# The first batch's q and k on one load queue, or on two

## The chip, the cores and the metric

The kernel runs on one core of one Trainium2 chip. A core has five engines that run side by side, each with its own instruction order: TensorE (PE, matmuls; its weight loads are listed as PEld), VectorE (DVE), ScalarE (ACT), GpSimd (POOL) and SyncE (SP), which here only issues transfers. Transfers between the main memory and the on-chip memory run on 16 DMA engines; SP and ScalarE each have a queue to them, called q1 and q10 in the profile. The metric is the device time of one execution in microseconds, the median of several.

## The reference

Linear attention with the map phi(x) = elu(x) + 1, and then a two-layer network with the tanh form of GELU:

```python
def phi(x):
    return np.where(x > 0, x, np.exp(x) - 1.0) + 1.0
q_p, k_p = (phi(q), phi(k))                       # q, k, v: 8 x 8 x 576 x 64, float32
kv = np.einsum('bhsd,bhse->bhde', k_p, v)
z = np.sum(k_p, axis=2)
num = np.einsum('bhsd,bhde->bhse', q_p, kv)
den = np.einsum('bhsd,bhd->bhs', q_p, z)[..., None] + 1e-06
x = num / den                                     # then heads side by side: 4608 x 512
h = x @ w_in                                      # w_in: 512 x 2048
g = 0.5 * h * (1.0 + np.tanh(c * (h + 0.044715 * h * h * h)))
return g @ w_out                                  # w_out: 2048 x 512
```

phi is computed as min(exp(x), max(x + 1, 1)): exp on ScalarE, the linear part and the minimum on VectorE.

## The kernel before

The order of instructions on each engine is the order in which the program names them; tiles come from pools, and an instruction waits for what it reads and for the tile it overwrites. Loads go through a pool of seven tiles (`pld`), so later loads wait until earlier tiles have been read.

The loads at the start, batch 0 first. Each of q and k comes in two halves:

```python
    def load_pairs(name, src, b, us=slice(0, NP), queue=nc.sync):
        s = src[b].rearrange("h s d -> (h s d)").rearrange("(u n f) -> n u f", n=P, f=J * D)
        queue.dma_start(out=ld[name, b][:, us, :], in_=s[:, us, :])

    def load_q_paired(b, parities=(0, 1)):
        src = q[b, :, 0:MAIN, :].rearrange("(u a) (p c) d -> p a u (c d)", a=2, c=C)
        for a in parities:
            nc.sync.dma_start(out=ld["q", b][:, NP * a : NP * (a + 1), :], in_=src[:, a])
    # ... cut ...
    halves = (slice(0, 2), slice(2, 4))
    for n in "qkv":
        ld_tile(n, 0)
    for s in range(2):
        load_q_paired(0, (s,))
        load_pairs("k", k, 0, halves[s], nc.scalar)
    nc.scalar.preload_act_table_set("exp_and_others")
    for s in range(2):
        load_pairs("v", v, 0, halves[s])
    for i in range(4):
        load_w(w_in_r, i)
    load_w(w_out_r, 0)
    # ... cut: batch 1's q, k and v, with w_out's other blocks between them, then batches 2 and 3 ...
```

A row of q's load is 256 floats (1 KB) long, a row of k's or v's 576 floats (2.3 KB).

The first batch, which fills the time until TensorE's main work can begin. `keep_warm` issues matmuls without use, to keep TensorE busy:

```python
    def first_batch():
        # ... cut ...
        keep_warm(18)
        for s in range(2):
            for n, hs in (("q", qs[s]), ("k", halves[s])):
                exp_of(n, 0, hs)       # ScalarE
                linear_of(n, 0, hs)    # VectorE, max(x + 1, 1)
                least_of(n, 0, hs)     # VectorE, the minimum
        transpose_q(0, nc.scalar.copy)
        keep_warm(10)
        transpose_q(1, nc.scalar.copy)
        keep_warm(2)
        for ii in range(2):
            cast_v_paired(0, halves[ii], nc.vector.tensor_copy)
        for ii in range(2):
            kv_ps = [bank("kv_ps", [P, E]) for _ in range(2)]
            kv_paired(0, ii, lambda a, ii: kv_ps[a])
            # ... cut: kv copied out of the accumulators by VectorE and ScalarE ...
        gelu_table()
        for s in range(2):
            cast_w_in(0, nc.gpsimd.tensor_copy, slice(256 * s, 256 * s + 256))
        for i in range(1, 4):
            cast_w_in(i, nc.gpsimd.tensor_copy)
        # ... cut: w_out's first blocks, then n, x, its transposes, and the first h quarters ...
```

Batch 1 is prepared while TensorE works on batch 0. In it stands the cast of the first part of w_out's last block, on VectorE, ahead of kv's copies:

```python
        def kv():
            kv_ps = [bank("kv_ps", [P, 2, E]) for _ in range(2)]
            for ii in range(2):
                kv_paired(b, ii, lambda a, ii: kv_ps[a][:, ii, :])
            cast_w_out(3, nc.vector.tensor_copy, slice(0, 1))
            for a, fn in enumerate((nc.vector.tensor_copy, nc.scalar.copy)):
                kv_evac(b, slice(2 * a, 2 * a + 2), kv_ps[a], fn)

        def last_w_out():
            cast_w_out(3, nc.scalar.copy, slice(1, 2))
            cast_w_out(3, nc.gpsimd.tensor_copy, slice(2, 4))
```

After that each batch is 16 blocks of h (`h_ps`, four matmuls each) with their GELU, and 16 groups of four matmuls into `o_ps`, with the next batch's attention between them.

Of the kernel before, what the change touches and what calls it, by code (L numbers as in the profile page):

```python
# [15 lines left out]
def kernel(  # L16
# [15 lines left out]
    nc = tc.nc  # L32
# [8 lines left out]
    NP = H // 2  # L41
# [40 lines left out]
    ld = {}  # L82
# [3 lines left out]
        shape = [P, NP, J * D] if b in PAIRED and name != "q" else [P, H, C * D]  # L86
        ld[name, b] = pld.tile(shape, FP32, name=name + "_x", tag="ld")

    def load_pairs(name, src, b, us=slice(0, NP), queue=nc.sync):
        s = src[b].rearrange("h s d -> (h s d)").rearrange("(u n f) -> n u f", n=P, f=J * D)  # L90
        queue.dma_start(out=ld[name, b][:, us, :], in_=s[:, us, :])

    def load_q_paired(b, parities=(0, 1)):
        src = q[b, :, 0:MAIN, :].rearrange("(u a) (p c) d -> p a u (c d)", a=2, c=C)
        for a in parities:
            nc.sync.dma_start(out=ld["q", b][:, NP * a : NP * (a + 1), :], in_=src[:, a])
# [45 lines left out]
    def cast_w_out(i, fn, ms=slice(0, 4)):  # L142
# [2 lines left out]
            in_=w_st[False, i][:, ms],  # L145
        )

    halves = (slice(0, 2), slice(2, 4))
    for n in "qkv":
        ld_tile(n, 0)  # L150
    for s in range(2):
        load_q_paired(0, (s,))
        load_pairs("k", k, 0, halves[s], nc.scalar)
    nc.scalar.preload_act_table_set("exp_and_others")
    for s in range(2):
        load_pairs("v", v, 0, halves[s])
    for i in range(4):
# [4 lines left out]
    load_w(w_out_r, 1)  # L162
    ld_tile("k", 1)
    load_pairs("k", k, 1)
    load_w(w_out_r, 2)
    ld_tile("v", 1)
# [581 lines left out]
```

## Time and profile before

| what | value |
|---|---|
| time, median of 3 | 289.38 us (289.31 to 289.49) |
| span of the profiled execution | 287.7 us, granted TensorE clock 1.000 |
| idle time of VectorE until the first q landed | 5.0 us |
| idle time of ScalarE for q's two landings | 3.8 us |
| transfers over the span | 53.76 MB, mean 187 GB/s |

The page's slices of 7.2 us each show how the time is divided. The digits are the busy share in tenths, the last line is the rate of transfers:

```profile
PE   8689999999999999999999999999999999999994
...
GB/s 241 407 407 396 410 400 263 348 219 153 184 231 279 228 174 167 380 148 139 204 296 202 79 257 349 106 78 169 34 49 30 88 66 0 50 92 6 0 73 73
```

TensorE is full from the fourth slice on. The transfers run at about 400 GB/s from the second slice to the sixth, that is to about 43 us: until then everything that is loaded lands one after the other at that rate, and later they are well below it.

### The profile page before, as it was taken

The numbers are of one execution on the slowest core, as the hardware profiler recorded it, in microseconds if no ns is written. First come the engines' busy times: TensorE is split into PE (matmuls) and PEld (weight loads), VectorE is DVE, ScalarE is ACT, GpSimd is POOL, SyncE is SP. The second block draws the span as 40 slices with busy tenths as digits, with TensorE's granted clock in tenths as the row PEclk, the third lists the DMA queues.
The fourth block names the chain that finished last, engine by engine and source line by source line (L and its number), as shares of the span: only waits on it lengthen the run. The fifth ranks groups of instructions, "written<-read, shape, count | busy, mean of one in ns | idle before, by whom it ended". The sixth has DMA issues, their size and how long they took to land.

```text
span 287.7 us, 4540 instructions
## 1 busy us (share of the span) xinstructions
PE 277.2 (96%) x1839; PEld 137.0 (48%) x1868; DVE 107.6 (37%) x180; ACT 164.5 (57%) x226; POOL 18.5 (6%) x25
## 2 busy tenths in 40 slices
PE   8689999999999999999999999999999999999994
PEld 3364455545445445544554455444544444444443
DVE  1950375733865283545146615540412010000001
ACT  3767896695975854585367735772562275027400
POOL 5067230000000000000000000000000000000000
PEclk9999999999999999999999999999999999999999
DMA  7999999965978888955799489825131220120022
GB/s 241 407 407 396 410 400 263 348 219 153 184 231 279 228 174 167 380 148 139 204 296 202 79 257 349 106 78 169 34 49 30 88 66 0 50 92 6 0 73 73
DMA packets 71379, 53.76 MB, mean 187 GB/s; under 512 B 42048, under 2 KB 62784, under 8 KB 71360
## 3 DMA queue, kind: packets, MB, share of 16 engines
q1 hardware_dynamic: 68112, 43.40, 54.1%
q10 hardware_dynamic: 3248, 10.09, 9.5%
q8 instruction: 14, 0.23, 0.3%
q14 instruction: 5, 0.04, 0.0%
HBM read 36.70 MB, written 9.44 MB: 160 GB/s over the span
## 4 chain that ended last, share of the span: by engine, by line
PE 92%; DVE 3%; DMA 2%; issue 1%; ACT 1%; DVEq 0%
PE o_ps L642 43%; PE h_ps L349 43%; PE n_ps L294 3%; DMA q_x<-in_q_dram 2%; PE kv_ps L278 1%; PE t_ps L341 1%; DVE k_p L236 1%; DVE q_p L236 0%; DVE k_p L223 0%; DVE vp L241 0%; PE kv_ps L263 0%; ACT q_e L212 0%; PE t_ps L469 0%; DVE x L330 0%; DVE x L309 0%
## 5 line engine op out<-in xcount | busy, mean ns | idle before, releaser
L642 PE MATMUL o_ps<-w_out_sb,g 128*128 128x512 bf16 (+1 forms) x581 | 126.3, 373 | 0.8 <-issue 0.2
L349 PE MATMUL h_ps<-xt,w_in_sb 128*128 128x512 bf16 (+1 forms) x556 | 116.7, 356 | 1.1 <-ACT xt L342 0.2
L359 ACT ACTIVATE g<-h_ps 128x512 bf16<-128x512 f32 x144 | 84.8, 597 | 46.8 <-PE h_ps L349 43.4
L642 PEld LDWEIGHTS <-g 128*128 128x128 bf16 x592 | 57.6, 98 | 65.2 <-issue 0.2
L349 PEld LDWEIGHTS <-w_in_sb 128*128 128x128 bf16 x636 | 57.4, 98 | 59.7 <-issue 0.9
L608 ACT COPY o_sb<-o_ps 128x512 f32<-128x512 f32 (+1 forms) x19 | 10.9, 575 | 61.3 <-PE o_ps L642 54.2
L608 DVE COPY o_sb<-o_ps 128x512 f32<-128x512 f32 (+1 forms) x18 | 12.1, 674 | 69.0 <-PE o_ps L642 69.0
L307 DVE RECIPROCAL r<-n_ps 128x8 f32<-128x8 f32 x34 | 7.1, 208 | 49.0 <-PE n_ps L294 49.0
L309 DVE TENSOR_TENSOR x<-n_ps,r 128x512 bf16<-128x512 f32 x34 | 23.5, 691 | 1.2
L212 ACT ACTIVATE q_e<-q_x 128x2048 bf16<-128x2048 f32 (+1 forms) x9 | 15.5, 1721 | 3.8 <-DMA q_x<-in_q_dram 3.8
L212 ACT ACTIVATE k_e<-k_x 128x2048 bf16<-128x2048 f32 (+2 forms) x9 | 15.8, 1751 | 0.0
L236 DVE TENSOR_TENSOR q_p<-q_p,q_e 128x2048 bf16<-128x2048 bf16 (+1 forms) x9 | 10.0, 1107 | 15.0 <-ACT q_e L212 14.9
L223 DVE TENSOR_SCALAR q_p<-q_x 128x2048 bf16<-128x2048 f32 (+1 forms) x9 | 9.9, 1101 | 14.7 <-DMA q_x<-in_q_dram 14.7
L349 PE MATMUL h_ps<-xt_rest,w_in_sb 128*128 128x512 bf16 x63 | 13.9, 379 | 0.1
L294 PEld LDWEIGHTS <-qt 128*128 128x128 bf16 x128 | 9.7, 98 | 7.2 <-DVE x L309 1.0
L223 DVE TENSOR_SCALAR k_p<-k_x 128x2048 bf16<-128x2048 f32 (+2 forms) x9 | 10.2, 1132 | 7.6 <-DMA k_x<-in_k_dram 7.6
L294 PE MATMUL n_ps<-kvbd,qt 128*128 128x130 bf16 x128 | 12.7, 221 | 0.0
L382 PE MATMUL w_ps<-warm 128*128 128x512 bf16 x31 | 9.5, 461 | 1.3 <-DVE warm L177 1.2
L236 DVE TENSOR_TENSOR k_p<-k_p,k_e 128x2048 bf16<-128x2048 bf16 (+2 forms) x9 | 10.2, 1133 | 0.8 <-ACT k_e L212 0.6
L373 ACT ACT_TABLE_LOAD x8 | 10.3, 1283 | 0.1
L212 ACT ACT_TABLE_LOAD x8 | 10.3, 1283 | 0.1
L290 DVE CAST kvbd<-kv_ps 64x260 bf16<-64x260 f32 (+2 forms) x18 | 6.6, 366 | 9.7 <-PE kv_ps L278 8.4
(49 smaller groups left out, 95.3 us busy)
## 6 DMA issues: line engine op xcount, KB each, us to landing
out_dram<-o_sb ACTq DMA_DIRECT2D x16, 512.0 KB, 3.3
q_x<-in_q_dram SPq DMA_DIRECT2D x6, 1024.0 KB, 6.4
k_x<-in_k_dram SPq DMA_DIRECT2D x6, 1024.0 KB, 11.3
v_x<-in_v_dram SPq DMA_DIRECT2D x6, 1024.0 KB, 8.0
w_st<-in_moe_w_in_dram SPq DMA_DIRECT2D x4, 1024.0 KB, 14.0
w_st<-in_moe_w_out_dram SPq DMA_DIRECT2D x4, 1024.0 KB, 13.3
q_x<-in_q_dram SPq DMA_DIRECT2D x4, 512.0 KB, 9.7
k_x<-in_k_dram ACTq DMA_DIRECT2D x2, 576.0 KB, 6.2
```

The lines of the kernel that those rows point to most:

```text
L212: nc.scalar.activation(by_chunk(exps[name, b], hs), x[:, hs].rearrange("p h (c d) -> p h c d", d=D), AF.Exp,)
L223: nc.vector.tensor_scalar(by_chunk(phi[name, b], hs), x[:, hs].rearrange("p h (c d) -> p h c d", d=D), 1.0, 1.0, op0=ALU.add, op1=ALU.max,)
L236: nc.vector.tensor_tensor(p, p, e, op=ALU.min)
L294: nc.tensor.matmul(ns[i // 2][rows, 2 * E * (i % 2) : 2 * E * (i % 2 + 1)], lhsT=qt_c[:, i, rows], rhs=kvbd[:, i, :], skip_group_check=True,)
L307: nc.vector.reciprocal(r, n_v[:, :, :, D])
L309: nc.vector.tensor_tensor(x_view(x, paired), n_v[:, :, :, 0:D], r[:, :, :, None].to_broadcast([P, 2, NP, D]), op=ALU.mult,)
L349: nc.tensor.matmul(h_ps[:, ts], lhsT=w_in_sb[:, c, P * m : P * (m + 1)], rhs=xt[:, c, ts], start=(c == 0), stop=(c == KM - 1), skip_group_ ...
L359: nc.scalar.activation(g[:, m, :], h_ps, AF.Gelu_apprx_tanh)
L373: nc.scalar.preload_act_table_set("gelu_apprx_tanh_and_others")
L382: nc.tensor.matmul(w_ps, lhsT=warm[:, 0:P], rhs=warm)
L608: (nc.scalar.copy if on_scalar else nc.vector.tensor_copy)(dst, src)
L642: nc.tensor.matmul(o_ps, lhsT=g[:, m, P * t : P * (t + 1)], rhs=w_out_sb[:, m, fs], start=(m == 0), stop=(m == MM - 1),)
```

## The change

In the kernel before, SP issues q's two halves while ScalarE issues k's two halves at the same time, on its own queue. In the changed kernel SP issues all four in turn: q's first half, k's first half, q's second, k's second. So the halves of q stand ahead of those of k in one queue, in the order in which they are mapped. ScalarE's first table load, which stood after its two issues, comes first on ScalarE. The description of the change also names the cast of w_out's last block on VectorE ahead of kv's copies; that part is the same in both kernels, and the diff does not touch it.

```diff
-    def load_pairs(name, src, b, us=slice(0, NP), queue=nc.sync):
+    def load_pairs(name, src, b, us=slice(0, NP)):
         s = src[b].rearrange("h s d -> (h s d)").rearrange("(u n f) -> n u f", n=P, f=J * D)
-        queue.dma_start(out=ld[name, b][:, us, :], in_=s[:, us, :])
+        nc.sync.dma_start(out=ld[name, b][:, us, :], in_=s[:, us, :])
 ...
+    nc.scalar.preload_act_table_set("exp_and_others")
     halves = (slice(0, 2), slice(2, 4))
     for n in "qkv":
         ld_tile(n, 0)
     for s in range(2):
         load_q_paired(0, (s,))
-        load_pairs("k", k, 0, halves[s], nc.scalar)
-    nc.scalar.preload_act_table_set("exp_and_others")
+        load_pairs("k", k, 0, halves[s])
     for s in range(2):
         load_pairs("v", v, 0, halves[s])
```

## The prediction

> **What bounds the kernel now.** I read the page first, then the chain of waits in its first 60 us, then VectorE's timeline there, then the DMA queues in short stretches. The page's busy times:
>
> ```profile
> PE 277.2 (96%) x1839; PEld 137.0 (48%) x1868; DVE 107.6 (37%) x180; ACT 164.5 (57%) x226; POOL 18.5 (6%) x25
> ```
>
> TensorE is busy 96% of the span, so at most about 10 us are not its own. From 53 us to the end the waits of PE sum to 0.2 us: nothing in this stretch can be gained or lost by an earlier transfer, it can only be shifted as a whole. The change touches loads of the first batch, so the question is what sets the moment at which TensorE starts its long unbroken run. The chain of waits in the first 60 us (start, length, what):
>
> ```profile
> 0.73 5.40 DMA q_x<-in_q_dram
> ...
> 6.16 1.06 ACT q_e L212
> ...
> 7.25 0.69 DVE q_p L236
> 7.94 0.68 DVE k_p L223
> ...
> 12.40 1.35 DVE vp L241 x2
> ...
> 13.79 0.48 PE kv_ps L263 x33
> ...
> 17.93 0.67 PE h_ps L349 x12
> ```
>
> The head is one chain: the first q half lands at 6.13 us, ScalarE takes its exp, then VectorE works with gaps of hundredths from 7.25 to 13.75 us, then kv, n, x, and the first h at 17.8. Every microsecond taken from it is one microsecond off the end, unless a transfer needed later holds it up. VectorE's timeline has the one wait that starts the chain, in brackets:
>
> ```profile
> 6.16 0.69 DVE L223 TENSOR_SCALAR q_p<-q_x 128x1024 bf16<-128x1024 f32 x1 [5.03 <-DMA q_x<-in_q_dram]
> 7.25 0.69 DVE L236 TENSOR_TENSOR q_p<-q_p,q_e 128x1024 bf16<-128x1024 bf16 x1 [0.40 <-ACT q_e L212]
> ```
>
> Why does q land so late? Of 6:6.5 us (queue: packets, MB, share of 16 engines; q1 is SP's queue, q10 ScalarE's):
>
> ```profile
> q10 hardware_dynamic: 61, 0.14, 70.9%
> q1 hardware_dynamic: 61, 0.06, 35.1%
> ```
>
> The same number of packets from either queue, but k's are 2.3 KB (0.14 MB / 61) and q's 1 KB, so q gets a third of the engines' time. The landings (issue start plus the median to landing in a stretch with one issue of the kind): k's first half 0.74 + 5.1 = 5.84, q's first 6.13, k's second 1.28 + 7.2 = 8.48, q's second 1.26 + 7.7 = 8.96, v's halves 1.79 + 8.6 = 10.4 and 2.34 + 9.5 = 11.84. Q is mapped first, but k lands first: k's packets push q back, and k then lies waiting (5.84, first used by ScalarE at 7.12).
>
> **What the Trainium skill says.** "DMA: Bandwidth & Descriptors", section "Queues, rings and completion order": each DMA engine goes round-robin between the queues that have work, packet by packet; within one queue it starts descriptors in order. The trace agrees: 61 against 61 packets above. The same page, "Issuing engines are not separate DMA queues": issuing from several engines saves only the issuing sequencer's time, since all run on the same 16 engines. The trace agrees: 399 GB/s with two queues (5.5 to 8 us), 409 GB/s with SP's alone (8.5 to 16 us). What ScalarE's queue saves is therefore SP's issue time, 0.48 us for a q half and about 0.5 for a k half.
>
> **The change part by part.** Nothing moves on PE, VectorE or GpSimd: their instruction orders are the same. ScalarE loses two issues (0.50 + 0.53 us), which it did at 0.74 to 1.81 while it had nothing to do, and its first table load (1.28 us, at 1.84 now) comes earlier; both lie before the first landing and are worth nothing. The part on w_out's last block stands in both kernels. SP issues q0, k0, q1, k1, v0, v1 in turn; v's and w_in's issues slip by two of some 0.5 us, about 1 us. An issue of about 0.5 us hands over about 0.55 MB, some 1 MB per us, over twice what the engines move, so SP's issue rate should not starve them.
>
> What changes is the order of landing. Bytes per boundary are the same, so each pair of halves is complete when it was before, but q's half comes first:
> - q0: SP's queue moved 23 + 112 = 135 of q0's 512 packets up to 3.2 us (stretches 1.7:2.2 and 2.2:3.2). The last 377 now share with nobody. SP's queue alone, with 1 KB packets, moved 256 in 24.3:25, 366 per us: 1.03 us, so the last packet at 4.23. The lag from last packet to landing: q1's packets sum to 450 up to 5.5 us, then 167 in 5.5:6, so q0's 512th went at 5.69 and landed at 6.13, lag 0.44. New landing 4.7; with a slower ramp 4.9. I take 4.85.
> - k0: when the pair is done, 6.13. q1: 512 / 366 = 1.40 us later, 7.55. k1: when the second pair was done, 8.96. v unchanged, 10.4 and 11.84.
>
> VectorE's order with those landings (durations from its timeline and the chain): q0 linear 4.88 to 5.57; exp of q0 on ScalarE to 5.94; minimum to 6.66; k0 linear to 7.34; exp of k0 6.16 to 7.31, minimum to 8.2; q1 linear to 8.8 (exp 7.6 to 8.66), minimum to 9.6; k1 linear to 10.3 (exp 9.0 to 10.15), minimum to 11.1; first v cast to 11.8; second v cast cannot start before v1's landing at 11.84, so 11.87 to 12.55. Now it ends at 13.75. Gain 1.20 us, where q's earlier landing alone gave 1.28.
>
> Then the transfers that could eat it:
> - w_in's first block lands at 14.49 (GpSimd's wait ends there) and its two casts end at 16.51. h starts at 17.77 now, 16.6 then: about 0.1 us of slack, and only the third h block needs the second cast.
> - k's second batch lands at 34.21 (VectorE). ScalarE's exp of it runs at 36.21, then 35.0: fits.
> - The last w_out block lands at 42.17. VectorE's order has it ahead of kv's copies:
>
> ```profile
> 42.17 0.43 DVE L143 CAST w_out_sb<-w_st 128x512 bf16<-128x512 f32 x1 [1.22 <-DMA w_st<-in_moe_w_out_dram]
> 43.67 0.60 DVE L290 CAST kvbd<-kv_ps 64x130 bf16<-64x130 f32 x2 [1.07 <-PE kv_ps L263]
> ```
>
> VectorE waits 1.07 us for kv after this cast. With kv 1.1 to 1.2 us earlier it waits for nothing: the copies start at 42.6 at the earliest, a gain of at most 1.07. GpSimd's half of that block is cast by 43.50, and o needs it at about 43.9. So 1.05 us survive, no more: this landing caps the gain. 289.38 - 1.05 = 288.33.
>
> **The rivals.**
> 1. *SP's queue alone starts slowly.* In 1.7:2.9 the engines moved 78 GB/s, from SP's queue alone, though q0 had been issued by 1.2; 400 came only when ScalarE's queue had joined. If SP's packets come slowly for another 2 us, at 185 per us, half the steady 366 (my assumption), q0 lands at 3.2 + 377/185 + 0.44 = 5.7 and 0.4 MB is lost, 1 us at 400 GB/s, on all later transfers. Then v1 lands near 12.8 and the last w_out block near 43.2: the gain is 0 to 0.2, or the time is up to 0.5 longer, 289.2 to 289.9. Against it: 5.5:6, where SP's queue had the engines nearly to itself for part of the stretch, shows 167 packets, 334 per us. A quarter.
> 2. *The gain is hidden by the later landings* (w_in's first block, or w_out's last): 0.3 to 0.8 us are left, 288.6 to 289.1. The slacks above are some 0.1 us and 0, so this is likely in part. A quarter.
> 3. *More than the sum*: with q and k in one queue the engines may fill sooner than at 3 us (ScalarE's packets began over a microsecond after SP's); all landings come up to 0.3 us earlier, the cap with them: 288.0. A tenth.
>
> **Range and chances.** The main sum 288.33, drawn a little up by the first two rivals: 288.4. From 287.9 (third rival, nothing lost) to 289.6 (first rival, mid-way). 2% would be 5.8 us; the whole wait for the first landing is 5.4 us, and no rival comes near. Faster by over 2%: 0.01; within 2%: 0.98; slower by over 2%: 0.01.
>
> **What would show it.** VectorE's first linear map should start at 4.7 to 4.9 (now 6.16); ScalarE should wait for DMA ahead of k's first exp and of q's second; the second v cast should end near 12.55, waiting on v's DMA; h should start near 16.6. VectorE's 1.07 us wait for kv near 43 us should be gone. From 53 us on, the same gaps as now, all about 1 us earlier. A first start at 5.7, or w_in's first cast later than 14.49, would speak for the first rival. I'd be wrong outright if GB/s before 6 us fell well below today's.

## The result and the profile after

The changed kernel takes 288.30 us (median of 6, 288.06 to 288.50) against 289.38 us before: a ratio of 0.9953, 95% interval 0.9932 to 0.9974. Run again beside a new set of runs of the kernel before (288.28 against 289.78 us), the ratio was 0.9948, interval 0.9936 to 0.9960. It is faster by about 1.1 to 1.5 us, 0.4 to 0.5%, and so within 2%. The prediction, 288.4 us between 287.9 and 289.6, was right.

The page's busy times after the change:

```profile
PE 276.6 (97%) x1839; PEld 137.1 (48%) x1868; DVE 107.8 (38%) x180; ACT 164.8 (58%) x226; POOL 18.4 (6%) x25
```

Every engine is busy as long as before, to 0.6 us or less; the span went from 287.7 to 286.2 us (286.6 in a second trace of the changed kernel). So what is gone is mostly waiting, and the question is where. VectorE's timeline (start, length in us, what, in brackets the wait ahead of it):

```profile
4.59 0.74 DVE L223 TENSOR_SCALAR q_p<-q_x 128x1024 bf16<-128x1024 f32 x1 [3.46 <-DMA q_x<-in_q_dram]
5.68 0.69 DVE L236 TENSOR_TENSOR q_p<-q_p,q_e 128x1024 bf16<-128x1024 bf16 x1 [0.35 <-ACT q_e L212]
...
10.79 1.63 DVE L241 CAST vp<-v_x 128x1152 bf16<-128x1152 f32 x2
```

Its wait for the first q is 3.46 us, where it was 5.03. And q's first half now crosses almost alone. The queue's view of 3.2 to 4 us (packets, MB, share of 16 engines):

```profile
DMA packets 299, 0.31 MB, mean 390 GB/s; under 512 B 4, under 2 KB 291, under 8 KB 299
...
q1 hardware_dynamic: 299, 0.31, 109.5%
```

The counts by size include the smaller ones, so 291 - 4 = 287 of these are rows of q (1 KB), 359 per us, and only 8 are longer: rows of k, which stand behind q in the queue. Before, SP's queue moved 105 packets in the same stretch and k's 85 longer rows took the rest.

The chain of waits of the first 60 us (start, length, what) no longer runs through VectorE's maps:

```profile
3.36 8.27 DMA v_x<-in_v_dram
...
11.66 0.77 DVE vp L241
...
12.47 0.48 PE kv_ps L263 x31
...
16.61 0.67 PE h_ps L349 x12
```

The second half of v, landing at 11.63 us, now starts the chain. The last v cast ends at 12.43 (it was 13.75), and the chain's first h is at 16.61 (it was 17.93): 1.32 us earlier. (The first h matmul itself, which the table below lists, starts at 16.45; it was 17.77.) The same 1.3 us are found at every step up to 56 us. VectorE near 42 us:

```profile
42.03 0.43 DVE L143 CAST w_out_sb<-w_st 128x512 bf16<-128x512 f32 x1 [1.79 <-DMA w_st<-in_moe_w_out_dram]
42.38 0.59 DVE L290 CAST kvbd<-kv_ps 64x130 bf16<-64x130 f32 x2
```

Before, there was a wait of 1.07 us for kv between these two lines. It is gone: the copies follow the cast at once. TensorE's first n of batch 1, which needs these copies, before and after:

```profile
44.35 0.40 PE L294 MATMUL n_ps<-kvbd,qt 128*128 128x130 bf16 x4
43.03 0.40 PE L294 MATMUL n_ps<-kvbd,qt 128*128 128x130 bf16 x4
```

It starts 1.32 us earlier, so the whole gain of the head has passed this place. From 53 us on TensorE waits 0.2 us in all, as before.

### The profile page after: what moved, and what is told of

Same layout as the page of the kernel before. It is cut to its first block, busy times and chain, and to the rows that moved or that the text cites. A ratio compares the mean times of both kernels' runs of the same rounds, so it can differ in the third digit from the quotient of the medians.

```text
span 286.2 us, 4541 instructions
## 1 busy us (share of the span) xinstructions
PE 276.6 (97%) x1839; PEld 137.1 (48%) x1868; DVE 107.8 (38%) x180; ACT 164.8 (58%) x226; POOL 18.4 (6%) x25
## 4 chain that ended last, share of the span: by engine, by line
PE 93%; DMA 3%; DVE 1%; issue 1%; SPq 1%; ACT 0%
PE o_ps L642 43%; PE h_ps L349 43%; PE n_ps L294 3%; DMA v_x<-in_v_dram 3%; PE kv_ps L278 1%; PE t_ps L341 1%; SPq L91 1%; PE kv_ps L263 0%; SPq L96 0%; PE t_ps L469 0%; DVE x L330 0%; DVE vp L241 0%; DVE x L309 0%; ACT xt L342 0%; PE w_ps L382 0%
## 5 line engine op out<-in xcount | busy, mean ns | idle before, releaser
L608 DVE COPY o_sb<-o_ps 128x512 f32<-128x512 f32 (+1 forms) x18 | 12.1, 674 | 69.0 <-PE o_ps L642 69.0
L236 DVE TENSOR_TENSOR k_p<-k_p,k_e 128x2048 bf16<-128x2048 bf16 (+2 forms) x9 | 11.0, 1227 | 0.8 <-ACT k_e L212 0.6
```

What stands on the lines that cost most here:

```text
L236: nc.vector.tensor_tensor(p, p, e, op=ALU.min)
L608: (nc.scalar.copy if on_scalar else nc.vector.tensor_copy)(dst, src)
```

## The experiments

Times are medians; ratios are to the kernel before, whose runs on the same chip stood beside each group of kernels: 289.78 us for the changed kernel again, k's half first, table load first and v on ScalarE's queue; 289.71 for the kernel before again, both q halves first and the two short heads; 289.66 for the last four. The ratios are not taken from the medians, so they can differ from the quotient of the medians by up to 0.0007.

| kernel | time, us | ratio (95%) | first h matmul, us |
|---|---|---|---|
| the kernel before, again | 289.82 | 0.9998 (0.9987 to 1.0010) | 17.93 |
| the changed kernel, again | 288.28 | 0.9948 (0.9936 to 0.9960) | 16.68 |
| k's half first, one queue | 290.20 | 1.0021 (1.0010 to 1.0032) | 18.29 |
| table load first, two queues | 289.89 | 1.0000 (0.9992 to 1.0007) | 18.22 |
| v on ScalarE's queue | 291.40 | 1.0060 (1.0039 to 1.0080) | 19.36 |
| both q halves first | 289.58 | 1.0000 (0.9984 to 1.0015) | 17.96 |
| short head | 288.24 | 0.9949 (0.9937 to 0.9961) | 16.53 |
| short head, copies first | 288.16 | 0.9945 (0.9933 to 0.9958) | 16.65 |
| pad in the changed kernel | 289.44 | 0.9994 (0.9986 to 1.0002) | 16.64 |
| pad in the kernel before | 289.92 | 1.0009 (1.0003 to 1.0016) | 18.19 |
| v split, copies first | 288.56 | 0.9962 (0.9949 to 0.9976) | 16.80 |
| copies first | 288.40 | 0.9961 (0.9948 to 0.9973) | 16.58 |

### Both kernels again

> The changed kernel once more, beside the others on the same chip: 1.0 to 1.4 us faster than before (ratio 0.995 to 0.9965), about 288.2 us; first h matmul near 16.45 us.

> The kernel before once more, for its trace beside the others on the same chip: ratio 1.0; first linear map at 6.1 to 6.6 us, first h near 17.8 to 18.2 us.

The kernel before came out as expected; the changed kernel's ratio of 0.9948 is just below the expected 0.995, and its first h came at 16.68 us, 0.2 later than expected. The traces give the size of what varies from one execution to the next: the first linear map starts at 6.16 and 6.32 us in the two traces of the kernel before, at 4.59 and 4.80 in the two of the changed kernel, and at 6.58 in the kernel before with a later load added (the pad below), whose head is the same. Differences of up to 0.4 us in a single landing are therefore not read below.

### Is it the order, or the single queue?

```diff
     for s in range(2):
-        load_q_paired(0, (s,))
         load_pairs("k", k, 0, halves[s])
+        load_q_paired(0, (s,))
```

> All four halves on SP's queue, but k's half ahead of q's each time; the maps keep their order, q first. Theory (what counts is that q's half lands first): q's first half lands when the pair is done, near 5.95 us as in the kernel before, and its second near 8.8; VectorE's chain then ends near 13.4 us, and most of the gain is gone: 288.9 to 289.3 us. Rival (one queue and earlier full use of the DMA engines bring the gain, whatever the order): within 0.2 us of the changed kernel, 288.1 to 288.5.

VectorE's timeline of this kernel:

```profile
5.87 0.69 DVE L223 TENSOR_SCALAR q_p<-q_x 128x1024 bf16<-128x1024 f32 x1 [4.74 <-DMA q_x<-in_q_dram]
...
9.61 0.69 DVE L223 TENSOR_SCALAR q_p<-q_x 128x1024 bf16<-128x1024 f32 x1 [0.42 <-DMA q_x<-in_q_dram]
10.69 0.69 DVE L236 TENSOR_TENSOR q_p<-q_p,q_e 128x1024 bf16<-128x1024 bf16 x1 [0.39 <-ACT q_e L212]
```

One queue is kept, only the order is turned round, and the whole gain is gone: 290.20 us, where the theory said 288.9 to 289.3 and the rival 288.1 to 288.5. The rival falls, although this kernel moved more bytes early: 93 rows of k, 0.21 MB, in 2 to 3 us, where the changed kernel moved 105 rows of q, 0.11 MB. The size was wrong: VectorE waits a second time, since q's second half lands near 9.6 us, 7.3 us after its issue, where I had 8.8. By 8.5 us this kernel had moved 2.3 MB (190, 382, 376 and 388 GB/s in the stretches that end at 3, 4, 6 and 8.5 us), more than the 2.2 MB of all four halves, and still 12 rows of q moved in 8.5 to 9 us, beside 84 longer rows, and 5 in 9 to 9.25 us. So rows of v, which stand behind q in the same queue, moved while rows of q were still owed. That the 16 engines had drifted apart would fit this; the trace's counts are not listed by engine, and the reason stays open.

### Is it the table load?

```diff
+    nc.scalar.preload_act_table_set("exp_and_others")
     halves = (slice(0, 2), slice(2, 4))
 ...
         load_pairs("k", k, 0, halves[s], nc.scalar)
-    nc.scalar.preload_act_table_set("exp_and_others")
```

> The kernel before with one part of the change alone: ScalarE's first table load ahead of its two k issues; k stays on ScalarE's queue. Rival (the earlier table load, not the queue, brings the gain): as the changed kernel, 288.2 to 288.4 us. Theory: the table load lies in ScalarE's idle time and brings nothing, 289.2 to 289.5 us; but if ScalarE's issues are held up until the table is loaded (1.28 us), k's packets come later, q's first half has the engines to itself for that long and lands near 5.0 us, and a part of the gain, 0.3 to 0.9 us, appears with the two queues kept.

The ratio is 1.0000 (0.9992 to 1.0007). ScalarE's first k issue starts at 0.77 us, during the table load, so it is not held up; q still shares with k and lands late (first map at 6.60 us). This part of the change is worth nothing.

### The suspected cost doubled

```diff
     for s in range(2):
-        load_pairs("v", v, 0, halves[s])
+        load_pairs("v", v, 0, halves[s], nc.scalar)
```

> The changed kernel with v's two halves issued from ScalarE's queue: the suspected cost doubled, since v's 2.3 KB packets now take turns with q's 1 KB and k's packets from the start. Theory: q's first half lands at 6.5 to 7.4 us, k's second at 10.5 to 11.6, first h at 18 to 19 us, 289.8 to 290.9 us. Rival (issuing from two queues saves issue time and so helps, or does nothing): 288.3 us or less.

(`load_pairs` has its queue argument again.) The queues in 4 to 4.5 us of this kernel:

```profile
q10 hardware_dynamic: 61, 0.14, 70.9%
q1 hardware_dynamic: 60, 0.06, 34.5%
```

This is the picture of the kernel before, with v in k's place: packet for packet, two thirds of the engines' time for the longer rows. Q's first half lands at 6.3 us, a little before the expected 6.5 to 7.4; k's halves land at 9.1 and 12.0 (2.30 + 9.7 to landing), the second later than the expected 10.5 to 11.6; and the time is 291.40 us, 3.1 us more than the changed kernel and even 0.5 above my upper bound. Issuing from two queues did not help; the longer rows on the second queue take the engines from what is needed first.

### Is q early enough by itself?

```diff
     for s in range(2):
         load_q_paired(0, (s,))
+    for s in range(2):
         load_pairs("k", k, 0, halves[s])
```

> The changed kernel with both q halves ahead of both k halves on SP's queue. From the landing sum: q at 4.6 to 4.8 and 6.1, k at 7.4 and 8.9 us; VectorE has the first k's linear part only at 7.4, its chain ends near 13.4, about 1 us later than in the changed kernel: 288.9 to 289.3 us. Rival (q early is all that counts): 288.3 us or less.

VectorE's timeline:

```profile
4.95 0.69 DVE L224 TENSOR_SCALAR q_p<-q_x 128x1024 bf16<-128x1024 f32 x1 [3.82 <-DMA q_x<-in_q_dram]
6.04 0.69 DVE L237 TENSOR_TENSOR q_p<-q_p,q_e 128x1024 bf16<-128x1024 bf16 x1 [0.40 <-ACT q_e L213]
7.71 0.76 DVE L224 TENSOR_SCALAR k_p<-k_x 128x1152 bf16<-128x1152 f32 x1 [0.97 <-DMA k_x<-in_k_dram]
8.90 0.76 DVE L237 TENSOR_TENSOR k_p<-k_p,k_e 128x1152 bf16<-128x1152 bf16 x1 [0.44 <-ACT k_e L213]
```

Q is early, but VectorE then waits 0.97 us for k and 0.44 us for its exp, and the time is that of the kernel before (ratio 1.0000; the expected 288.9 to 289.3 was 0.3 us too low). The first h is at 17.96, against 17.93 us. So the rival "q early is all that counts" falls: of the three orders tried on one queue, only that of the maps brings the gain.

### Does the landing of w_out's last block cap the gain?

A first attempt shortened the head by force. v's second half of the first batch is loaded behind w_in's blocks, its cast is left out, and kv's second part multiplies ones in its place, so this kernel no longer computes the reference:

```diff
-    for s in range(2):
-        load_pairs("v", v, 0, halves[s])
+    load_pairs("v", v, 0, halves[0])
     for i in range(4):
         load_w(w_in_r, i)
+    load_pairs("v", v, 0, halves[1])
 ...
-        nc.gpsimd.memset(vps[i][:, :, D:E], 1.0)
+        nc.gpsimd.memset(vps[i] if i == 0 else vps[i][:, :, D:E], 1.0)
 ...
-        for ii in range(2):
-            cast_v_paired(0, halves[ii], nc.vector.tensor_copy)
+        cast_v_paired(0, halves[0], nc.vector.tensor_copy)
```

> The changed kernel with a head shortened by force: v's second half of the first batch is loaded only behind w_in's four blocks and its cast is left out (kv's second part then multiplies ones, so the output is not the reference's); the bytes loaded up to w_out's last block stay the same. Both theories: first h 0.7 to 0.95 us earlier than in the changed kernel, near 15.6 us. Theory (w_out's last block, landing near 42 us, caps the gain): TensorE catches it and idles near 42 us; the time is that of the changed kernel within 0.3 us, 287.9 to 288.4. Rival (no cap, the head passes on to the end): 287.3 to 287.6 us.

In the second version batch 1's kv copies also come first (the diff stands further down):

> As the short head, and in batch 1 VectorE copies kv out ahead of its cast of w_out's last block. If VectorE's order is what the landing holds up, n starts earlier and only GpSimd's cast of the block (done near 43.35 us) still stops o: 0.3 to 0.5 us faster than the short head alone. If the landing acts through GpSimd's cast alone, no difference (under 0.1 us).

Both are inconclusive. The times are inside what the theory said (288.24 and 288.16 us, 0.08 apart), but for another reason: the head did not get shorter, first h at 16.53 and 16.65 us. In the first of them kv's two parts ran in one go, so their copies came one behind the other (12.59 to 13.55 us), and one of VectorE's linear maps took 1.15 us in place of 0.69, at a time when GpSimd was still on the memsets that the longer one had pushed back (whether these two hang together was not tried). A head that is no shorter tests no cap.

So I moved the landing in place of the head: 512 KB that nobody reads are loaded ahead of w_out's last block, in either kernel:

```diff
     load_pairs("v", v, 1)
+    pad = const.tile([P, 2, 512], FP32, name="pad")
+    nc.sync.dma_start(out=pad, in_=w_out_r[:, 0:2, :])
     load_w(w_out_r, 3)
```

> The changed kernel with a load of 512 KB that nobody reads, ahead of w_out's last block, which so lands 1.3 us later (512 KB at 400 GB/s), near 43.4 us; the head stays as it is. Theory (the landing of w_out's last block caps the gain, and no slack is left before it): 1.0 to 1.4 us slower than the changed kernel, which is about the time of the kernel before, ratio 0.9985 to 1.001. Rival (TensorE has slack there, no cap): as the changed kernel, ratio 0.994 to 0.9965.

> The same load of 512 KB in the kernel before. There VectorE waited 1.07 us for kv behind its cast of the block, so the pad should take up that slack and cost only about 0.2 us: ratio 1.0 to 1.002. If the pad costs the full 1.3 us here too (ratio 1.0045), its cost has nothing to do with the slack that the change used up.

VectorE in the changed kernel with the pad:

```profile
43.20 0.43 DVE L143 CAST w_out_sb<-w_st 128x512 bf16<-128x512 f32 x1 [3.10 <-DMA w_st<-in_moe_w_out_dram]
43.55 0.59 DVE L292 CAST kvbd<-kv_ps 64x130 bf16<-64x130 f32 x2
```

and what TensorE waited for after 17 us there:

```profile
PE n_ps L296 <- DVE kvbd L292: 0.8, 1, 0.8
```

The head is untouched (first h at 16.64 us), and still the gain is all but gone, 0.9994: TensorE reaches n and waits 0.8 us for kv's copies, which stand behind the cast. (Against the second trace of the changed kernel the landing moved by 43.20 - 42.28 = 0.92 us, not by my 1.3. The ratio moved by 0.0046, which is 1.3 us with an uncertainty of about 0.4; the trace's span grew by 0.7.) In the kernel before the same pad costs 0.0009 x 289.7 = 0.26 us. VectorE there:

```profile
43.60 0.43 DVE L143 CAST w_out_sb<-w_st 128x512 bf16<-128x512 f32 x1 [2.23 <-DMA w_st<-in_moe_w_out_dram]
44.09 0.60 DVE L292 CAST kvbd<-kv_ps 64x130 bf16<-64x130 f32 x2
```

The copies start 0.49 us after the cast, 0.14 more than the 0.35 of a copy that follows directly. In the second trace of the kernel before, without the pad, these lines are:

```profile
42.21 0.43 DVE L143 CAST w_out_sb<-w_st 128x512 bf16<-128x512 f32 x1 [1.10 <-DMA w_st<-in_moe_w_out_dram]
43.83 0.60 DVE L290 CAST kvbd<-kv_ps 64x130 bf16<-64x130 f32 x2 [1.20 <-PE kv_ps L263]
```

That is a slack of 43.83 - 42.21 - 0.35 = 1.27 us, and a landing 1.39 us later has eaten it. (The trace with the pad keeps 0.14 us of it only because its head was slow: its first h came at 18.19 us, not at 17.93. So the pad's cost of 0.26 us cannot be read off that one trace.) Two kernels that differ by 1.5 us without the pad differ by 0.4 to 0.5 us with it (289.44 and 289.92, or 0.9994 and 1.0009). The rival of no cap falls: the kernel before had about a microsecond of slack at this landing, and the change has used it up.

### More than that?

The order in batch 1 alone, kv's copies ahead of the cast:

```diff
-            cast_w_out(3, nc.vector.tensor_copy, slice(0, 1))
             for a, fn in enumerate((nc.vector.tensor_copy, nc.scalar.copy)):
                 kv_evac(b, slice(2 * a, 2 * a + 2), kv_ps[a], fn)
+            cast_w_out(3, nc.vector.tensor_copy, slice(0, 1))
```

> The changed kernel with only the order in batch 1 undone: kv copied out ahead of VectorE's cast of w_out's last block (the part that the description names and both kernels have). In the changed kernel that cast ends within 0.1 us of kv's end, so the order should matter little: within 0.2 us of the changed kernel, ratio 0.9945 to 0.996.

And with the second v cast of the first batch shared with ScalarE:

```diff
-        for ii in range(2):
-            cast_v_paired(0, halves[ii], nc.vector.tensor_copy)
+        cast_v_paired(0, halves[0], nc.vector.tensor_copy)
+        cast_v_paired(0, slice(2, 3), nc.vector.tensor_copy)
+        cast_v_paired(0, slice(3, 4), nc.scalar.copy)
```

> A try for more: the changed kernel with the second v cast of the first batch split between VectorE and ScalarE (the head now waits for that landing and cast), and in batch 1 kv copied out ahead of VectorE's cast of w_out's last block. The head should gain 0.2 to 0.35 us (first h near 16.2 to 16.4 us, where the changed kernel has 16.45 to 16.68); with GpSimd's cast of the last block done near 43.4 us, 0.1 to 0.3 us of it may reach the end: 287.9 to 288.2 us, ratio 0.9938 to 0.9948.

The order alone gave 0.9961, the changed kernel 0.9948 and 0.9953 with intervals that overlap it: no difference is shown, and none was expected (0.9945 to 0.996). So the cast ahead of kv's copies, which cost 0.8 us under the pad, costs the changed kernel nothing that can be measured. The split brought nothing either: 0.9962 where 0.9938 to 0.9948 was expected, with first h at 16.80 us where 16.2 to 16.4 was. ScalarE's timeline shows one reason (start, length, what):

```profile
10.22 1.99 ACT L395 COPY qt<-t_ps 128x1024 bf16<-128x1024 bf16 x2
12.10 0.69 ACT L241 CAST vp<-v_x 128x576 bf16<-128x576 f32 x1
```

ScalarE is busy with q's transposes until 12.1 us and does its share only then, to 12.79: no earlier than VectorE would have finished alone. The other is VectorE's own share. It started at 11.98 us, when v's second half had landed, and took 0.754 us for 128x576 elements, as long as the 0.756 us of a cast of 128x1152, so halving it saved nothing. Why is not shown. No version beats the changed kernel.

## Why the prediction was right

- *Q's landing.* Predicted 4.85 us for the first half; measured 4.53 (0.73 + 3.8), and VectorE's first map at 4.59, 4.80 in the second trace. The cause, k's rows taking turns with q's, is shown from two sides: take the order away and keep the one queue, and the gain is gone; put v's rows beside q's, and it is worse than before.
- *The other landings.* k's first half 6.13 predicted, 5.96 measured; q's second 7.55 (its sum, 6.13 + 1.40, gives 7.53) and 7.29; k's second 8.96 and 8.80; v's second 11.84 and 11.63. All were 0.15 to 0.3 us early in the first trace; in the second, v's last cast starts at 11.89, on the predicted number.
- *The head.* Gain predicted 1.20 us, limited by v's second landing; measured 1.32 in the first pair of traces and 17.93 - 16.68 = 1.25 in the second. The chain of waits after the change starts at that landing, as predicted.
- *The cap.* This term was mis-sized. 1.05 us were to survive; VectorE's copies came 43.67 - 42.38 = 1.29 us earlier, 43.83 - 42.63 = 1.20 in the second pair, and TensorE's first n of batch 1 came 1.32 and 1.24 us earlier. That is the whole gain of the head: the landing of w_out's last block took nothing from it. The pads show that it would take the next part, but I put the cap too low. I let the copies wait for the whole 0.43 us of the cast ahead of them; the next instruction starts 0.35 us after the cast does, in this trace and in the second (42.28 and 42.63). And in the first trace the block landed 0.14 us earlier.
- *The number.* The traces gained about 1.3 us in the head, and the times 1.1 us in the first set of runs and 1.5 in the second, against a predicted 1.05. Both the head's gain and what passes the cap were put too low, so that the first median lies within 0.1 us of the prediction is in part luck.
- *The parts worth nothing.* ScalarE's table load, measured alone: 1.0000.
- *The rivals.* The slow start of SP's queue alone did not happen: 389 GB/s in 3 to 4 us and 326 in the second trace, against 350 and 367 with two queues, where the rival's 185 rows of 1 KB per us would be about 190. That the later landings hide a part did not happen here: the slack at w_out's last block was just enough. The third, engines that fill sooner, is not clear: w_in's first block was cast from 14.32 in place of 14.49 us in one pair of traces, from 14.56 in place of 14.64 in the other, no more than two executions differ by.

## What to carry to other kernels

In these runs a second issuing queue brought no bytes: 397 GB/s in 4 to 8 us with two queues, 401 with one. It only decided whose bytes came first, and turns by packet favoured the queue with the longer rows (61 packets from each in 6 to 6.5 us, 0.14 MB against 0.06). So put what is consumed in order into one queue in that order, and look for every load in flight beside it on another. Before counting a gain at the head of a kernel, find the next fixed landing down the line and the wait behind it: that wait is about the most that can pass through. Here it was 1.07 us as listed, and 43.67 - 42.17 - 0.35 = 1.15 counted from start to start.

## What the runs showed of the hardware that I had not expected

- In these traces a copy of VectorE whose operands were ready started 0.35 us after the start of a cast listed at 0.43 us (42.03 and 42.38, 42.28 and 42.63, 43.20 and 43.55). A chain summed from listed lengths comes out too long by such overlaps.
- With k's half ahead of q's in one queue, q's second half landed 7.3 us after its issue, near 9.6 us, although by 8.5 us as many bytes had moved as all four halves hold. The last 17 of q's rows came after that, so the mean rate did not give the landing.
- Rows came at about the same number per us at the start, whatever their length: 105 of 1 KB from 2 to 3 us in the changed kernel, 93 of 2.3 KB with k first.
